# Layer norm statistics finished on GpSimd, and normalized tiles transposed by DMA, in a one-core transformer block

## The chip, the cores and the metric

The kernel runs on one core of a Trainium2 chip. The time is device microseconds (us) of that core for one execution. TensorE is called PE, VectorE DVE, ScalarE ACT, GpSimd POOL and SyncE SP, as in the profile.

## What is computed

One block of an adaptive layer norm transformer over 2048 tokens of width 512, in bf16. Six vectors come from a conditioning vector; the first half is a sliding-window attention of 32 heads of width 16 with a window of 256 tokens, the second half an MLP that mixes over tokens.

```python
mod = (silu(c) @ w_mod).reshape(1, 6, 1, -1)            # sa, ca, ga, sb, cb, gb
h = layernorm(x) * (1 + ca) + sa                        # eps 1e-5 under the root
q, k, v = split_heads(h @ wqkv)                         # 32 heads of 16
p = softmax(where(0 <= i - j < 256, q @ k.T * 16**-0.5, -1e9))
x = x + ga * ((p @ v) @ wo)
h = layernorm(x) * (1 + cb) + sb
h = layernorm(h)
u = gelu(einsum('bsd,sf->bdf', h, w1) + b1)             # f = 1792, sums over tokens
x = x + gb * (einsum('bdf,fs->bds', u, w2) + b2).T
```

## The kernel before, in words

The 2048 tokens lie in 16 tiles of 128 tokens by 512 features (`xres`, tile x in the profile). They form four groups G of four tiles. For each group the kernel does three things.

**Projection** (`proj0` for group 0, `proj(G)` from line 875 for groups 1 to 3). `norm_ops` (line 621) takes the statistics of the four tiles: for each tile a BATCH_NORM_STATS2 and a BATCH_NORM_AGGREGATE on DVE, which leave mean and variance in mv; then, for the batch of four, two ACT instructions that make rs = exp(-0.5 ln(var + eps)); then, where `shifted` is set, one DVE instruction for nm = -mean * rs. `normalize` (line 653) makes xn = x * rs + nm on POOL. Then `e_tr` (line 909) transposes xn on PE, 16 blocks of 128x128 for a group, into two PSUM tiles pt, and `e_h` (line 919) evicts them with scale and shift of the modulation into h1T, four instructions of 128x512, on ACT or DVE. There is one h1T, so a group's transposes stand behind the last projection matmul of the group before (`before`). Projection matmuls give pq, pk, pv; DVE or ACT evicts these to QT, kb and vb, and POOL spreads kb and vb into KT and VT with masks.

**Attention** (`attention`, line 1166). 75 chunks of scores. A chunk is 512 columns for each of four heads: scores on PE into pss (three heads, 1536 columns) and psb (the fourth), two exponentials on ACT into et (128x1536 and 128x512), a mask product on DVE, and products with VT and with ones on PE into po. ACT makes the reciprocal of the sums (two instructions on lz), and DVE the product OT. Seven et tiles form a ring.

**Post** (`post`, line 1058). The output projection pa, the sum with x, and the two layer norms of the second half (tags l2 and l3) with the modulation between them, down to hb, the input of the MLP. Groups 0 to 2 take batches of four tiles and normalize on POOL; group 3 takes two batches of two tiles on DVE.

The MLP's first matmul sums over tokens. For the first eight tiles it is done during attention (`partials`, line 1128: 14 sums of eight matmuls, kept in part), for the other eight in `tail` (line 1332); the second matmul py follows (line 1398). The first halves of w1 (seven transfers of 512 KB, tiles w1p) are loaded together once the modulation's tiles are released; the second half of a pair is loaded into the same tile when the first is used up. w2 (14 transfers of 512 KB, w2r) goes into the room that attention leaves. All these transfers are issued in order by SP.

**What sets the order.** Each step is an `Op` with engines, a cost and a place `pos`. `run_schedule` (line 157) is a list scheduler that runs when the program is built: it picks, step by step, what can start first by the costs written in the code, and emits it; each engine then runs its instructions strictly in that order. The table `MOVED` shifts the place of each step, `CHOSEN` pins some steps to an engine, and a few constants set tolerances. Three PSUM banks (od0 to od2) are shared by all matmul results except the scores. Nearly every instruction is recorded with one source line, L321, that of the helper `wrapped`, so the profile is read by tile names.

Of the kernel before, what the change touches and what calls it, by code (L numbers as in the profile page):

```python
# [9 lines left out]
ACT = mybir.ActivationFunctionType  # L10
# [49 lines left out]
    70, 4467, 3352, 236, -2676, 456, 1177, 4380, -3616, 1904, 51, -1450, 1581, 958, 823, -389, -5421, -5059, 1961,  # L60
    2253, 438, -1893, -2821, 945, -1140, -4188, -353, -2060, -2167, -978, 2785, -3149, 1766, 1833, 1121, 397, -1610,
    2266, -135, 1589, -377, 7177, -547, -1613, 2278, 49, -3915, -2041, 1444, 697, 2329, 335, 842, -1466, -1538,
    1377, -5151, -700, -1478, -1297, -2245, -1441, -577, -782, -322, 1149, 2468, -1282, -23, -9, -2034, -1112,
    -2090, -625, 418, 4015, -42, 441, -1267, 2114, -2423, -17, -1812, 180, 3007, -20, -127, 802, 3660, -1718, -5323,
    3891, -7996, 648, -157, -307, -3897, 3154, -248, -205, -746, -758, -341, -1065, -1027, -4094, -1115, -563, 774,
    -567, 919, -3068, -612, 3429, -533, -2943, -2732, -468, 0, 0, 0, -2833, 0, 0, 0, 4012, 0, 0, 0, 2087, 0, 0, 0,
    -2967, 0, 0, 0, 1896, -3625, -4555, -4396, -1330, -4146, -5997, 945, -4357, -2281, -2265, -4078, -3736, -2234,
    -2238, -2088, -5933, -6820, -1831, -3919, -86, 0, 0, 0, 2917, 0, 0, 0, -3397, 0, 0, 0, -3869, -126, -4012,
    -3163, -3098, -2291, -4626, 0, 0, 0, -3744, 0, 0, 0, -1255, -4473, -1567, -5495, -1964, -1985, 265, 0, 0, 0,
    918, 0, 0, 0, -4777, 0, 0, 0, 1884, -2580, -2329, -6050, -3851, -5651, 256, 0, 0, 0, -5949, 0, 0, 0, -4823,  # L70
    -7822, -188, -4690, -2183, -263, 1168, -1223, 183, -640, -1307, -1147, -1714, -1455, -1506, -2586, 369, 1115,
    1706, -2188, -2861, 3663, 4317, -1900, -3694, -32, 3684, -759, -1106, 3652, 3201, 467, 894, -202, 3287, -1972,
    1847, -2954, -7238, 4109, 577, -2623, 1009, 1661, 161, -2100, 101, -2459, -3002, 5002, -912, -1539, -2952, -188,
    -1212, -4900, -1081, -1401, -1012, -4700, -847, -478, -927, -4723, 4, -2646, -2959, 1376, -2654, 2541, -1668,
    1670, -4531, 263, 242, -1454, -761, 5658, 701, -1595, -1229, 6812, 142, 3436, -1137, -1827, 1368, -8297, -973,
    4089, 270, -301, 1175, 1887, 356, -1883, 3294, 2057, -2871, -6721, 1015, -3531, 3626, -577, 0, 0, 0, 2127, 0, 0,
    0, -2754, 0, 0, 0, -4673, 943, -6490, -2346, -6169, 6023, -570, 0, 0, 0, -2772, 0, 0, 0, -4887, -5214, -7251,
    -5132, -1166, -2049, -1760, 0, 0, 0, -1967, 0, 0, 0, -5431, 0, 0, 0, -3239, -3416, -1061, -5548, -213, 83,
    -2126, 0, 0, 0, 3863, 0, 0, 0, -4984, -5944, -9389, -5675, -2048, -16, -1222, 0, 0, 0, -5372, 0, 0, 0, 2682, 0,
    0, 0, -617, -2090, -6144, -7478, -6129, -2188, -1303, 0, 0, 0, 696, 0, 0, 0, -1038, -2636, -6267, -1648, -1777,  # L80
    2198, 1755, 0, 0, 0, 492, 0, 0, 0, -1432, 0, 0, 0, -1277, -2134, -6449, -2845, -3570, -2232, -1708, 0, 0, 0,
    -6073, 0, 0, 0, 1239, -2264, -6809, -228, -8212, -689, -989, -6426, -3078, 2186, 337, -1300, 1261, -2087, -2761,
    893, 177, -1261, 2307, 1095, -2051, 2155, 1484, -718, -1829, -3249, 2311, -1384, 4273, -2313, 3194, -1649, 1588,
    1454, 5130, -530, -710, -982, 2509, -101, -180, 1765, 2456, 1338, 1123, -3497, 463, 3176, 4783, -112, -2629,
    -3687, -4796, -2110, 1941, 3875, -3895, -2150, -1119, 511, 1867, 2651, -2030, 286, -1797, 2014, -2735, -3109,
    -6218, 5379, -1878, -1972, 2969, 669, -1488, -1885, 5494, 5382, 2803, 1178, 419, 210, 665, -1845, -2987, -1371,
    -2546, -79, 502, 2421, -3740, -3509, -4120, 3194, 1449, 2377, 7205, 1978, -4180, 1689, 328, 595, 861, -1145, 0,
    0, 0, -1748, 0, 0, 0, -3812, 0, 0, 0, -852, -2397, -8784, -7079, -5062, -2663, -5549, 0, 0, 0, -1775, 0, 0, 0,
    -2167, -4070, 1863, -11014, 1648, -2508, -3414, 0, 0, 0, -9171, 0, 0, 0, 1351, 0, 0, 0, -3992, -8907, -294,
    -2896, -1484, -1986, -3310, 0, 0, 0, -1995, 0, 0, 0, -8063, -3126, 497, -7719, -3726, -818, -3217, 0, 0, 0,  # L90
    -2662, 0, 0, 0, -2304, 0, 0, 0, -2693, -3688, -2743, -9195, -2877, -2467, -3147, 0, 0, 0, 596, 0, 0, 0, -1887,
    -9586, -8234, -8156, -458, -1239, -6090, 0, 0, 0, -1663, 0, 0, 0, 529, 0, 0, 0, -935, -8603, 1013, -8474, -4906,
    5740, -3352, 0, 0, 0, -1917, 0, 0, 0, -180, -5566, -5089, -12042, -481, 6294, -3974, -1183, -3266, -178, -1697,
    -6917, -619, -5490, -2874, 2307, -5558, -1283, -4286, 97, 688, 6764, -1, -1859, -415, 3548, 1772, -4681, 1128,
    -2098, -2960, 1273, -1577, -163, 2239, 2964, 5783, 4456, -4137, -1579, 46, 0, -1588, 934, -546, -666, -3967,
    922, 13, 3137, 4633, 2039, 3624, 1927, -1697, 1288, 2451, 2284, 960, -220, 1747, -1705, 1834, -14, -324, -1715,
    930, 5465, 2964, 3593, 1371, 13, -2362, 3398, 338, -227, -500, 2508, 2181, -2169, 2677, -444, 743, 735, 1245,
    255, -2098, 430, 1563, -3647, 2858, 1753, 2806, 527, -3215, 2354, 512, 815, -1559, -5022, 401, -899, 2225, -711,
    0, 0, 0, -3379, 0, 0, 0, -8261, 0, 0, 0, -3454, -2109, -10884, -12007, -4125, -741, -1625, 0, 0, 0, -8786, 0, 0,
    0, -2529, -1969, 877, 2220, -3540, -689, -4323, 0, 0, 0, -2887, 0, 0, 0, 3442, 0, 0, 0, 1147, -506, -4707, 243,  # L100
    -4008, 4990, 538, 0, 0, 0, -1551, 0, 0, 0, 801, 2579, -669, -851, 595, -1406, -3620, 0, 0, 0, 1957, 0, 0, 0,
    4432, 0, 0, 0, -592, -548, -329, -509, -4812, 2495, -5021, 0, 0, 0, -6650, 0, 0, 0, -1072, 1375, -5880, -5071,
    -2736, 3118, 1549, 0, 0, 0, 2386, 0, 0, 0, -3661, 0, 0, 0, 477, 1221, -1627, -2365, -361, 5951, 594, 0, 0, 0,
    2506, 0, 0, 0, 3581, -1001, 1296, 176, 420, 397, 324, -4889, -2563, -1105, -2612, -2591, -604, -599, -862, 1146,
    -1278, 2218, -1316, 2057, 3521, 4902, -1209, -814, 1554, -2807, -2931, -1068, 3534, -141, -4935, -918, 93,
    -4825, 5353, 376, 1479, 227, -286, 525, -4654, 286, -1945, -1026, -5792, 2309, -1932, 2357, -6381, -4690, -6370,
    2678, 1440, -1714, -5050, 2763, 2858, -5925, -3043, 29, 2732, 665, -5900, 1821, 446, 1510, -2919, -7548, -1921,
    1301, 2643, 494, -5402, -1795, 1683, 1622, 2097, -6974, -1007, 1550, 1919, 2660, 71, -1309, 1458, 2205, -6599,
    826, -804, 1417, 1615, -4471, 2083, -3678, 1073, 3010, 1306, 433, -3422, 1315, 1609, -1032, -411, 78, 1524,
    1477, -6392, -434, 3787, 1105, 5774, -5290, 1101, -1493, -4202, 968, 1042, -54, -172, -4572, -3764, 2523, -765,  # L110
    2726, 2606, 5637, -466, 2597, 3103, 823, 5349, 4113, -246, 101, 1017, -4325, -5010, 4065, 5501, -473, 1661,
    -3058, 2980, -6736, 4775, -848, 3670, 2893, 1742, 2902, -1577, 4555, 2286, 3783, 2751, 1785, 1240, -4116, 3712,
    -1835, 5125, 2811, 1922, -734, -3129, 2641, -2571, 5041, -405, -1849, 1660, -1257, 3386, -2559, 1378, -2067,
    182, -112, -909, 3526, -424, 1530, 2954, -307, 2441, -3570, 3799, 3287, -2833, 2974, -2740, 1418, -1497, 4010,
    -5506, 2265, -2370, -187, 4427, -970, 2987, 4216, 210, -2930, 1810, 1023, 5420, 3094, 6105, 3490, 2010, -2298,
    -2949, -4217,
]
CHOSEN = {
    "ACT": [
        80, 91, 111, 116,  # L120
    ],
    "DVE": [
        65, 73, 75, 78, 83, 87, 100, 106, 109, 114, 276, 280, 287, 295, 299, 310, 313, 317, 498, 501, 516, 520, 528,
        542, 723, 726, 737, 748, 752, 767, 938, 943, 953, 958, 968, 973, 978, 998,
    ],
}
S_TOL = 0.154
E_TOL = 0.474
LATE = 2.695
BATCH = True  # L130
HORIZON = 202.566
STICK = 5.96
AV_POS = 0.2
LZ_POS = 0.0
M_POS = -0.5
OT_POS = -1.0
FINE = 0.0


# [140 lines left out]
def kernel(  # L280
# [340 lines left out]
    def norm_ops(tag, tiles, deps, poss, key, shifted):  # L621
# [27 lines left out]
        if shifted:  # L649
            o = op(f"{tag}nm", "DVE", 0.12, e_nm, deps=[o], pos=poss[-1])  # L650
# [793 lines left out]
```

## Time and profile before

| | |
|---|---|
| time, median of 3 runs (lowest to highest) | 264.41 us (264.3 to 265.02) |
| time of the profiled execution | 264.88 us |
| its span, first to last instruction | 263.1 us |
| first exponential starts, last one ends | 12.9 us, 181.8 us |
| first matmul of py starts | 211.1 us |

The profile lists, for each engine, busy time, groups of like instructions (count, busy us, mean ns), what ended an engine's idle time, and a chain of waits that leads back from the last instruction. Instructions of one engine overlap a little at their ends, so the sum of means is somewhat above the busy time, and the distance from one start to the next is what an instruction really takes from its engine. Three stretches are told apart below: up to 13 us (loads, modulation, first projection), 13 to about 180 us (attention with all else beside it), and the rest (the MLP).

### The profile page before, as it was taken

Reading aid. Unit: us, or ns where it says so; the run is one execution under the profiler, and the core shown is the slowest. Engines: PE = TensorE matmul, PEld = TensorE weight load, DVE = VectorE, ACT = ScalarE, POOL = GpSimd, SP = SyncE. Lnnn points to the kernel's source line nnn. Section 1 sums busy time; section 2 is a strip of 40 time slices with the busy share of each in tenths; the row PEclk is TensorE's granted clock in tenths of the full one; section 3 lists DMA queues with packets and bytes.
Section 4 is the critical chain, followed back from the end, with each engine's and each line's share of the span. In section 5 each row is a group of like instructions: output and inputs, shape, how many; then the busy total and the mean of one; then the engine's idle time right before and its main releaser. Section 6 shows DMA issues by size and latency. Waiting matters only on the chain.

```text
span 263.1 us, 8290 instructions
## 1 busy us (share of the span) xinstructions
PE 238.3 (91%) x3568; PEld 130.6 (50%) x3605; DVE 209.9 (80%) x438; ACT 183.5 (70%) x273; POOL 91.3 (35%) x129
## 2 busy tenths in 40 slices
PE   8889879899986898878899999999999999999994
PEld 2666556554654444444644444446444444444441
DVE  3799999998999989999856979789778864444443
ACT  3499999999998998998999999997226620000000
POOL 5069903970796692387840051050000000000000
PEclk9999999999999999999999999999999999999999
DMA  7999100099000000000002022222699501111111
GB/s 220 319 350 235 4 4 2 3 278 264 23 4 2 2 2 2 2 2 1 5 2 82 1 82 82 85 80 82 229 383 386 201 23 40 41 40 55 47 40 40
DMA packets 33261, 24.66 MB, mean 94 GB/s; under 512 B 5064, under 2 KB 29640, under 8 KB 33224
## 3 DMA queue, kind: packets, MB, share of 16 engines
q1 hardware_dynamic: 32800, 23.74, 29.9%
q8 instruction: 28, 0.46, 0.7%
q10 hardware_dynamic: 424, 0.39, 0.4%
q14 instruction: 9, 0.07, 0.1%
HBM read 22.03 MB, written 2.10 MB: 92 GB/s over the span
## 4 chain that ended last, share of the span: by engine, by line
DVE 39%; PE 33%; ACT 16%; issue 7%; DMA 3%; SPq 0%; DVEq 0%
PE py L321 18%; ACT et L321 13%; PE pu L321 10%; DVE et L321 10%; DVE st L321 7%; DVE h L321 4%; DVE vb L321 3%; DVE kb L321 3%; ACT lz L321 2%; DVE OT L321 2%; DVE QT L321 2%; DVE x L321 2%; DVE h1T L321 2%; DMA x<-in_A_x_dram 2%; PE po L321 2%
## 5 line engine op out<-in xcount | busy, mean ns | idle before, releaser
L321 ACT ACTIVATE et<-pss 128x1536 bf16<-128x1536 f32 x75 | 109.4, 1458 | 3.6 <-PE psb L321 2.7
L321 DVE TENSOR_TENSOR et<-et,maskt 128x1024 bf16<-128x1024 bf16 (+1 forms) x79 | 49.6, 635 | 6.9 <-ACT et L321 6.5
L321 PE MATMUL pu<-hb,w1p 128*128 128x512 bf16 x212 | 50.2, 380 | 1.0 <-issue 0.8
L321 PE MATMUL py<-guT,w2r 128*128 128x512 bf16 x220 | 48.3, 379 | 0.2
L321 ACT ACTIVATE et<-psb 128x512 bf16<-128x512 f32 x75 | 45.5, 607 | 0.0
L321 POOL TENSOR_SCALAR KT<-kb,mask_par 128x512 bf16<-128x512 bf16 (+1 forms) x38 | 27.5, 736 | 37.0 <-DVE kb L321 36.9
L321 PE MATMUL pss<-QT,KT 32*128 32x64 bf16 (+3 forms) x720 | 29.9, 230 | 7.6 <-ACT et L321 4.7
L321 PEld LDWEIGHTS <-w2r 128*128 128x128 bf16 x224 | 21.9, 98 | 26.4
L321 PE MATMUL po<-et,VT 128*32 128x64 bf16 (+3 forms) x960 | 32.0, 234 | 3.0 <-DVE kb L321 2.1
L321 POOL TENSOR_SCALAR xn<-x,rs,nm 128x512 bf16<-128x512 bf16 x24 | 24.0, 1006 | 28.5 <-DVE nm L321 26.1
L321 PEld LDWEIGHTS <-w1p 128*128 128x128 bf16 x224 | 20.2, 98 | 24.9 <-issue 2.4
L321 PE MATMUL po<-et,ones_bd 128*32 128x256 bf16 (+3 forms) x624 | 31.4, 268 | 0.0
L321 DVE TENSOR_TENSOR otile<-py,xr 128x512 bf16<-128x512 f32 x16 | 11.1, 692 | 25.5 <-PE py L321 25.5
L321 PEld LDWEIGHTS <-KT 32*128 32x128 bf16 x960 | 16.6, 92 | 28.5 <-issue 25.5
L321 PE MATMUL psb<-QT,KT 32*128 32x64 bf16 (+3 forms) x240 | 29.3, 231 | 0.0
L321 POOL TENSOR_SCALAR VT<-vb,mask_half 128x512 bf16<-128x512 bf16 x32 | 25.9, 823 | 5.9 <-DVE vb L321 5.4
L321 PEld LDWEIGHTS <-VT 128*32 128x32 bf16 x960 | 20.3, 96 | 10.6 <-issue 7.8
L321 DVE BATCH_NORM_STATS2 st<-x 128x6 f32<-128x512 bf16 x32 | 22.0, 686 | 3.1 <-DMA x<-in_A_x_dram 2.8
L321 PEld LDWEIGHTS <-wqkv 128*128 128x128 bf16 x164 | 14.1, 97 | 16.7 <-issue 8.2
L321 PE MATMUL pk<-h1T,wqkv 128*128 128x256 bf16 (+1 forms) x98 | 19.7, 319 | 2.2 <-DVE QT L321 1.7
L321 PE MATMUL pv<-wqkv,h1T 128*64 128x256 bf16 x256 | 17.2, 275 | 1.1 <-DVE h1T L321 0.5
L321 PE MATMUL pa<-wod,OT 128*128 128x512 bf16 x57 | 15.9, 381 | 0.7 <-DVE wod L321 0.2
(83 smaller groups left out, 288.5 us busy)
## 6 DMA issues: line engine op xcount, KB each, us to landing
w1p<-in_B_w_dram SPq DMA_DIRECT2D x14, 512.0 KB, 5.7
w2r<-in_B_w_dram SPq DMA_DIRECT2D x14, 512.0 KB, 10.8
wmod<-in_w_mod_dram SPq DMA_DIRECT2D x4, 512.0 KB, 8.3
out_dram<-otile SPq DMA_DIRECT2D x16, 128.0 KB, 1.7
x<-in_A_x_dram SPq DMA_DIRECT2D x15, 128.0 KB, 5.2
wqkv<-in_A_wqkv_dram SPq DMA_DIRECT2D x4, 256.0 KB, 5.4
wmod<-in_w_mod_dram SPq DMA_DIRECT2D x3, 256.0 KB, 4.5
wqkv<-in_A_wqkv_dram SPq DMA_DIRECT2D x1, 512.0 KB, 5.8
```

The costliest lines, as they stand in the source:

```text
L321: ins = call(*args, **kwargs)
```

## The change

Five things change together.

1. In batches of four tiles (`quiet`: tag l1 of groups 1 to 3, tags l2 and l3 of groups 0 to 2, nine batches) DVE does only BATCH_NORM_STATS2. The aggregate, the two ACT instructions and nm are gone; seven small POOL instructions on 128x4 or 128x8 make mean and 1/sqrt(var + eps) out of the raw statistics, the last by a power of -1/2. `normalize` then does (x - mean) * rs, still one POOL instruction.
2. In groups 1 to 3 the transposes on PE and the evictions are gone. Four DMA transposes of 128x512, issued by SP, write h1T, and `e_h` applies scale and shift in place in SBUF, on DVE or POOL. There are two h1T tiles, used by turns, so a group waits for the projection two groups before.
3. The loads of w1's first halves are seven steps of their own, each placed by the scheduler, and so are the loads of the second halves.
4. `warm` moves to another pool, three small memsets are added on POOL, some buffer counts change.
5. The tables `MOVED` and `CHOSEN` and the scheduler's constants are replaced, so the order of the instructions on all engines is a new one.

```diff
-    def norm_ops(tag, tiles, deps, poss, key, shifted):
+    def norm_ops(tag, tiles, deps, poss, key, quiet):
...
-            st = small.tile([P, nc.vector.BN_STATS_DIM], F32, name="st", tag=tag + "st")
-            ve.bn_stats(out=st[:], in_=tiles(i)[:])
-            ve.bn_aggr(out=box[key][0][:, i, :], in_=st[:])
+                box[key] = new("st", 6), new("mv", 2), new("rs")
+            st, mv = box[key][0][:, i, :], box[key][1][:, i, :]
+            ve.bn_stats(out=st, in_=tiles(i)[:])
+            if not quiet:
+                ve.bn_aggr(out=mv, in_=st)
+
+        def e_ag(e):
+            st, mv, rs = box[key]
+            sq = small.tile([P, n], F32, name="sq", tag=f"sq{n}", bufs=2)
+            po.tensor_tensor(out=mv[:], in0=st[:, :, 1:3], in1=st[:, :, 4:6], op=ALU.add)
+            po.tensor_tensor(out=mv[:], in0=mv[:], in1=halves[:, 0:n, :], op=ALU.mult)
+            po.tensor_tensor(out=sq[:], in0=st[:, :, 1], in1=st[:, :, 4], op=ALU.subtract)
+            po.tensor_tensor(out=sq[:], in0=sq[:], in1=sq[:], op=ALU.mult)
+            po.tensor_scalar(out=sq[:], in0=sq[:], scalar1=0.25, scalar2=EPS, op0=ALU.mult, op1=ALU.add)
+            po.tensor_tensor(out=sq[:], in0=sq[:], in1=mv[:, :, 1], op=ALU.add)
+            po.tensor_tensor(out=rs[:], in0=sq[:], in1=power[:, 0:n], op=ALU.pow)
...
-        def e_nm(e):
-            mv, rs, nm = box[key]
-            ve.scalar_tensor_tensor(out=nm[:], in0=mv[:, :, 0], scalar=-1.0, in1=rs[:], op0=ALU.mult, op1=ALU.mult)
...
-        o = op(f"{tag}rs", "ACT", 0.45, e_rs, deps=st_ops, pos=poss[-1])
-        if shifted:
-            o = op(f"{tag}nm", "DVE", 0.12, e_nm, deps=[o], pos=poss[-1])
-        return o
+        if quiet:
+            return op(f"{tag}ag", "POOL", 2.0, e_ag, deps=st_ops, pos=poss[-1])
+        return op(f"{tag}rs", "ACT", 0.45, e_rs, deps=st_ops, pos=poss[-1])
...
-            a = op("tr", "PE", 0.27, lambda e, f=e_tr: f(0), deps=xn_ops[0:2], pos=p_tr, cls="D", alloc="od", behind=before)
-            z = op("tr", "PE", 0.27, lambda e, f=e_tr: f(1), deps=xn_ops[2:4] + [a], pos=p_tr, cls="D")
-                h = op("h1T", {"ACT": 1.0, "DVE": 0.9}, 0.9, e_h, deps=[z, o_fm] + before, pos=p_tr)
+        h1T = h1Ts[r2]
+        before = [proj_last[G - 2]] if G >= 2 else []
...
+        def e_xt(e, i):
+            dma.dma_start(out=h1T[:, :, i * P : (i + 1) * P], in_=xn[i][:], transpose=True)
...
+            xt_ops.append(op("xt", "SP", 1.25, lambda e, i=i: e_xt(e, i), deps=xn_ops[-1:] + before, pos=p_ln + 2.5, extra=XT_AFTER))
...
+                for dc in (2 * dp, 2 * dp + 1):
+                    ENGINE[e].tensor_scalar(
+                        out=h1T[:, dc, :], in0=h1T[:, dc, :], scalar1=scale, scalar2=shift, op0=ALU.mult, op1=ALU.add,
+                    )
+            h_ops.append(op("h1T", {"POOL": 1.85, "DVE": 0.66}, 0.9, e_h, deps=xt_ops + [o_fm], pos=p_tr))
...
-        for pair in range(NF // 2):
-            load_w1(pair, 0)
...
+            loaded.append(op("w1l", "SP", 1.35, lambda e, n=n: load_w1(n, 0), deps=loaded[-1:] or [opened],
+                             pos=start_of(1) + 3.0 + 2.0 * n, extra=W1_AFTER))
...
-                if fc % 2 == 1:
-                    load_w1(fc // 2, 1)
...
+            if fc % 2 == 1:
+                second[fc // 2] = op("w1h", "SP", 1.35, lambda e, fc=fc: load_w1(fc // 2, 1), deps=[g], pos=pos + 0.5, extra=W1_AFTER)
```

## The prediction

> **What bounds the kernel now.** First the busy time by stretches: start and end, length, then busy us of PE, PE's weight loads, DVE, ACT and POOL.
>
> ```profile
> 13.00:140.00 127.00, 110.56 (x2319) 68.37 (x2338) 118.66 (x246) 121.84 (x176) 79.76 (x98) 1.00 0.24 62
> 140.00:180.00 40.00, 38.19 (x700) 19.71 (x710) 34.34 (x74) 39.70 (x58) 7.93 (x8) 1.00 0.26 74
> 180.00:211.00 31.00, 30.61 (x258) 14.92 (x251) 26.21 (x59) 15.53 (x29) 0.00 (x0) 1.00 0.74 265
> 211.00:263.00 52.00, 48.44 (x222) 21.83 (x224) 23.13 (x36) 1.27 (x2) 0.00 (x0) 0.99 0.12 41
> ```
>
> From 13 to 180 us ACT is busy for 161.5 of 167 us: this stretch is as long as ACT's work plus 5.5 us. DVE comes second (118.7 of 127 up to 140). After 180 PE works without a gap, and its clock row reads full. So the time is a start of 13 us, ACT's work, and a run of PE at the end. What ended ACT's idle time inside the stretch (us, times, longest):
>
> ```profile
> ACT et L321 <- PE psb L321: 2.7, 6, 0.8
> ACT rs L321 <- DVE mv L321: 0.7, 2, 0.5
> ACT lz L321 <- PE po L321: 0.6, 2, 0.4
> ```
>
> Little of it is anyone's fault; the work itself has to go. The groups by shape (count, busy us, mean ns, idle before):
>
> ```profile
> L321 ACT ACTIVATE rs<-mv,eps_t 128x4 f32<-128x4 f32 x9 | 2.9, 317 | 0.7 <-DVE mv L321 0.7
> L321 ACT ACTIVATE rs<-rs 128x4 f32<-128x4 f32 x9 | 1.9, 206 | 0.3
> L321 DVE BATCH_NORM_AGGREGATE mv<-st 128x2 f32<-128x6 f32 x48 | 8.7, 182 | 1.7
> L321 DVE TENSOR_SCALAR h1T<-pt,modFM 128x512 bf16<-128x512 bf16 x12 | 5.9, 534 | 0.0
> L321 DVE SCALAR_TENSOR_TENSOR nm<-mv,rs 128x4 f32<-128x4 f32 x9 | 1.9, 213 | 1.1 <-ACT rs L321 1.1
> L321 POOL COPY maskt<-tmpm 64x64 bf16<-64x64 bf16 x6 | 1.3, 250 | 0.0
> ```
>
> The first two rows are the change's target on ACT: 18 instructions of four columns each, 4.8 us. What they take from ACT is read from starts in the timeline:
>
> ```profile
> 172.52 0.35 ACT L321 ACTIVATE rs<-mv,eps_t 128x4 f32<-128x4 f32 x1
> 172.90 0.21 ACT L321 ACTIVATE rs<-rs 128x4 f32<-128x4 f32 x1
> 173.01 1.43 ACT L321 ACTIVATE et<-pss 128x1536 bf16<-128x1536 f32 x1
> ```
>
> The pair begins at 172.52 and the next exponential at 173.01: 0.49 us.
>
> **The change, part by part.**
>
> *ACT.* Nine pairs go: 9 x 0.49 = 4.4 us. In the changed order three evictions QT of 128x256 (386 ns by their row) stand on DVE and not on ACT; instructions of this size start 0.27 us apart (lz at 161.43, the next at 161.70), so 0.8 us more. ACT's work falls by **5.2 us**, nearly all of it ahead of the 54th exponential (136.5 us). The order of scores and exponentials is otherwise the same, and the count of partial sums ahead of the last scores too (102 matmuls before, 98 after).
>
> *DVE.* 36 of the 48 aggregates go (36 x 0.182 = 6.6), nine nm (1.9) and the twelve evictions of pt (12 x 0.534 = 6.4). Added are three QT of 128x256 (1.2 us at 0.40) and eight in-place products on h1T, the other four being on POOL. That shape and pair of operations stands in the row xn of group 0 at 428 ns; 406 is its value without POOL beside it, and 918 the slowest DVE instruction on 128x512 in SBUF (one wod). I take 428: 3.4 us, within 3.2 to 7.3. Sum: -6.6 - 1.9 - 6.4 + 1.2 + 3.4 = **-10.3 us**, or -6.4 at the worst. DVE falls well behind ACT, so none of this counts by itself; it hides the added work and may take some of ACT's 5.5 us of idle time.
>
> *PE.* 48 transposes go: by the row of pt (56 in 4.8 us) 4.1 us. PE is 87% busy up to 140, so this too is relief, not gain.
>
> *POOL.* 9 x 7 small instructions. Nothing in the trace has this size on POOL but memsets of 128x2 (102 ns) and the copy of 64x64 (250 ns), and no power at all; ends are 63 x 0.10 = 6 us and, at the 554 ns of KT on 128x256, 35 us. I take 250, the nearest with an input: 15.8 us, 1.75 us a batch. With four h1T at 841 ns (KT of 128x512) POOL gains 19 us, 15.7 of them up to 140: 95 of 122 us busy. POOL has the room. Behind each batch stand the spreads KT and VT, which PE waits for; but the path from the last statistics to xn gets no longer, since it loses the wait in ACT's queue (24.49 rs, 25.13 nm).
>
> *DMA transposes.* No row shows one. Each moves 128 KB. The nearest: stores of 128 KB land after 1.7 us, loads of x of 128 KB after 5.2 beside other traffic, and SP needs 0.37 us to issue one. In the stretch where group 1 needs them the DMA row of the page reads 1, then 0, so I stay near the stores: 2.5 us each, overlapping; ends are 1.7 us for all and 4 x 5.2 in a row. Before, xn of group 1 runs on POOL from 29.59 to 33.04 and h1T from 35.43 to 37.6; with 2.5 us the last tile lands at about 36, so nothing changes. Groups 2 and 3 have more air: h1T in two copies lets their transposes run a group earlier. On SP they stand behind b2b (issued by 26.1) and ahead of the first loads of w1 (51.5), which partial sums need only after 120 us.
>
> The Trainium skill's page DMA: Bandwidth & Descriptors (Latency and other measured facts; Anatomy of one DMA) gives 261 GB/s for transposes and about 2 us fixed; by these an estimate is 0.5 + 2.0 = 2.5 us, and no run here shows it yet. The sum stays as it is.
>
> *The start.* Three memsets (0.1 us each) precede the identity on POOL; DVE waits 2.8 us for x there, which hides them. *The end.* In the changed order the second half of the last w1 pair is issued behind all 14 loads of w2, where before it was third. Before, the first w2r goes out at 184.94, when the last po is done, and fifteen transfers of 0.52 MB at the page's 383 GB/s take 20.5 us. PE has 106 matmuls, 0.219 us each (49 in 10.74), between the last po and the first that reads this tile: 23.2 us. It just fits, so 0 us.
>
> **Sum.** The profiled execution took 264.9 us (its span 263.1 and 1.8 around it). Less 5.2 of ACT's work and 0.3 of its 0.7 us of waits for mv: 259.4. The median lies 0.5 below the profiled execution, so **259.0 us**. Kept idle time on ACT is my choice: it could fall by up to 5 us, with DVE relieved, or rise.
>
> **Rivals.**
>
> *More than the work.* With 10 us less on DVE and 4 on PE the waits for psb, pss and po (3.8 us) go too: 255.5. Against it: PE is the one waited for there, and its order with the new transposes is no simpler.
>
> *GpSimd slows DVE.* The products with bc_sb on tile h, all of one shape:
>
> ```profile
> L321 DVE TENSOR_TENSOR h<-h,bc_sb x13: 424/714/880, 73.2 to 179.7; 128x512 bf16<-128x512 bf16 x13
> ```
>
> They take 424 ns at least and 880 at most, and the long ones (0.80 at 73.17, 0.88 at 75.50) lie while POOL runs xn and VT; POOL's KT in turn needs 690 to 1197 ns. POOL's share up to 140 rises from 63% to 78%: some 80 products in SBUF on DVE, 0.15 more of them covered, 0.37 us each: 4.4 us, of DVE's 10.3. DVE keeps 6 us of relief, so ACT should stay the limit; but DVE ran at 98% up to 56 us, and there stalls may eat half the gain: 261.7. The Trainium skill speaks against this change here: GPSIMD Engine Reference (Performance versus the Vector engine; Key points) holds elementwise work on GpSimd to be about twice as slow and in contention with VectorE; the trace agrees on the contention.
>
> *The last tile of w1 is late.* If w2 lands at 300 GB/s, or its issue is held by the queue, PE waits at the end: fifteen transfers take 26 us, 3 more than PE has: 262.
>
> *Slower: group 1 stalls.* In the changed order the four in-place products of group 1 stand together in DVE's queue, waiting for all four transposes; masks, OT and evictions to free the three PSUM banks queue behind them. If transposes run one after another at 5.2 us, the last lands at 30.4 + 21 = 51 and not 37, and DVE stands for 13 us in a stretch where it has no slack. The same holds if the batch of seven takes many us on POOL. Group 1's first scores come at 48, its keys are ready at 41.9, so up to 5 us are absorbed; the rest, 8 us or more, is lost: 267. It decides from about 3.3 us a transpose in a row. For it: nothing here shows a transposing transfer; against it: no traffic beside them, and stores of the same size land in 1.7 us.
>
> **How the numbers follow.** Forecast (257 to 261) 0.60; more than the work 0.07; GpSimd slows DVE 0.12; late w1 tile 0.07; group 1 stalls 0.14. The likeliest gives 259.0. From 256.0 to 263.7 lie all but the last and some of the second: 0.82. A measurement of this kernel tells 0.3%, 0.8 us, from no change. Faster is the first four, less 0.05 that ends within 0.8 us of 264.4: 0.80; with 0.01 of the last, same is 0.06; slower 0.14.
>
> **What would show it.** Right: ACT has no rs of 128x4, its busy time falls by 6 and the last exponential ends near 176.5; DVE falls by about 10; POOL rises by 15 to 25. Transposes: landing under 3 us, no wait of DVE's h1T for DMA over 1 us. The end: no wait of PE's pu for w1p. Wrong: idle ACT over 7 us up to the last exponential, DVE's masks and h much longer than now, or h1T waiting.

## The result, and the profile after

The changed kernel takes **293.3 us** (median of 4 runs, 293.14 to 294.45) where the kernel before takes 264.36 beside it: a ratio of 1.110, interval 1.107 to 1.113. Forecast were 259.0 us, with a range up to 263.7; the forecast has the wrong sign and misses by 34 us. Where a kernel has executions over 1.5% above its fastest one, a median below is over all its executions and a ratio over the others. The profiled execution took 293.41 us, its span 291.7, and the mean clock of TensorE is 0.952 where it was 0.999.

The same stretches as before, columns as there (PE, PEld, DVE, ACT, POOL, then clock, DMA share, GB/s):

```profile
13.00:140.00 127.00, 102.52 (x2028) 60.02 (x2044) 106.72 (x199) 105.99 (x141) 120.82 (x141) 0.95 0.31 74
140.00:180.00 40.00, 34.25 (x636) 17.17 (x637) 22.70 (x42) 33.29 (x46) 21.17 (x21) 0.91 0.15 42
```

POOL, busy 79.8 us of the first 127 before, is now busy for 120.8, while ACT stands at 106 where it was at 121.8. POOL is now the busiest engine up to 140 us. The chain of waits, by engine, says the same; before it held no POOL at all (DVE 39%, PE 33%, ACT 16%):

```profile
POOL 39%; PE 31%; DVE 14%; DMA 7%; issue 4%; ACT 3%; POOLq 1%; SPq 0%
```

What ended ACT's idle time (us, times, longest); the three rows answer to those for psb, po and pss before, which had 0.8 us at the longest:

```profile
ACT et L322 <- PE psb L322: 19.1, 10, 6.1
ACT lz L322 <- PE po L322: 11.8, 6, 7.3
ACT et L322 <- PE pss L322: 5.9, 1, 5.9
```

These are 37 us in 17 waits. Sixteen of them, 29.5 us, lie ahead of the last exponential, which ends at 202.6 us, 20.8 later than before. The longest, 7.3 us, lies behind it: POOL makes four hb from 198.1 to 206.8, a matmul pu waits 3.8 us for them, and the last products po are queued behind pu. The first matmul of py starts at 239.8, 28.7 later.

What POOL does with its time, by shape (count, busy us, mean ns, idle before), first the kernel before, then the changed one:

```profile
L321 POOL TENSOR_SCALAR xn<-x,rs,nm 128x512 bf16<-128x512 bf16 x24 | 24.0, 1006 | 28.5 <-DVE nm L321 26.1 <-DVE h L321 2.5
L321 POOL TENSOR_SCALAR hb<-h,rs,nm 128x512 bf16<-128x512 bf16 x12 | 10.8, 909 | 13.9 <-DVE nm L321 13.9
```

```profile
L322 POOL TENSOR_SCALAR xn<-x,mv,rs 128x512 bf16<-128x512 bf16 x24 | 53.4, 2230 | 0.2
L322 POOL TENSOR_SCALAR hb<-h,mv,rs 128x512 bf16<-128x512 bf16 x12 | 25.4, 2127 | 0.2
L322 POOL TENSOR_TENSOR rs<-sq,power 128x4 f32<-128x4 f32 x9 | 10.0, 1111 | 0.7
```

The rows xn and hb matter most: the 36 normalizations of the same tiles go from means of 1006 and 909 ns to 2230 and 2127. They have the same shape, the same engine and the same operation name; POOL spends 44 us more on them. The rows of the small instructions add up to 23.6 us, the power being the largest.

The clock falls where PE stands still. A gap in PE's work and the stretches behind it, columns as above:

```profile
124.00:126.00 2.00, 0.00 (x0) 0.00 (x0) 0.70 (x1) 1.22 (x2) 2.00 (x3) 1.00 0.00 0
126.00:128.00 2.00, 0.00 (x0) 0.00 (x0) 1.97 (x5) 0.00 (x0) 2.00 (x2) 0.82 0.00 0
130.00:132.00 2.00, 2.00 (x50) 1.27 (x52) 2.00 (x4) 0.93 (x1) 2.00 (x2) 0.50 0.00 0
```

How POOL's lateness gets to PE is seen in the timeline, DVE first:

```profile
125.30 0.91 DVE L322 TENSOR_TENSOR h<-xn,bc_cb 128x512 bf16<-128x512 bf16 x1 [4.33 <-POOL xn L322]
127.90 0.67 DVE L322 CAST QT<-pq 128x512 bf16<-128x512 f32 x1
```

```profile
128.62 1.01 PE L322 MATMUL pk<-h1T,wqkv 128*128 128x512 bf16 x2 [4.84 <-DVE QT L322]
```

DVE stands 4.3 us ahead of a product on xn that POOL is still making; the eviction QT, whose matmul was long done, is queued behind it, and PE's next matmuls wait for QT. Then PE works for some 5.5 us at half of the clock. So a long wait such as this one is paid a second time.

### The profile page after: what moved, and what is told of

The parts are those of the page before. It is cut to its first block, busy times and chain, and to the rows that moved or that the text cites. A ratio compares the mean times of both kernels' runs of the same rounds, so it can differ in the third digit from the quotient of the medians.

```text
span 291.7 us, 8238 instructions
## 1 busy us (share of the span) xinstructions
PE 245.9 (84%) x3518; PEld 129.0 (44%) x3557; DVE 205.2 (70%) x392; ACT 179.1 (61%) x252; POOL 161.4 (55%) x199
## 4 chain that ended last, share of the span: by engine, by line
POOL 39%; PE 31%; DVE 14%; DMA 7%; issue 4%; ACT 3%; POOLq 1%; SPq 0%
PE py L322 17%; POOL xn L322 12%; PE pu L322 9%; POOL hb L322 8%; POOL VT L322 5%; POOL KT L322 5%; DMA w1p<-in_B_w_dram 4%; DVE st L322 3%; POOL rs L322 3%; DVE et L322 3%; POOL sq L322 3%; DVE h L322 3%; PE po L322 3%; ACT et L322 2%; DMA x<-in_A_x_dram 2%
## 5 line engine op out<-in xcount | busy, mean ns | idle before, releaser
L322 PE MATMUL pu<-hb,w1p 128*128 128x512 bf16 x213 | 55.1, 401 | 10.4 <-POOL hb L322 7.9
L322 POOL TENSOR_SCALAR xn<-x,mv,rs 128x512 bf16<-128x512 bf16 x24 | 53.4, 2230 | 0.2
L322 PE MATMUL pss<-QT,KT 32*128 32x64 bf16 (+3 forms) x720 | 31.2, 236 | 11.1 <-POOL KT L322 4.7
L322 PE MATMUL po<-et,VT 128*32 128x64 bf16 (+3 forms) x960 | 34.1, 243 | 6.9 <-DVE part L322 2.2
L322 PEld LDWEIGHTS <-w1p 128*128 128x128 bf16 x224 | 20.9, 101 | 37.9 <-issue 15.5
L322 PE MATMUL po<-et,ones_bd 128*32 128x256 bf16 (+3 forms) x624 | 32.8, 280 | 0.0
L322 POOL TENSOR_SCALAR KT<-kb,mask_par 128x512 bf16<-128x512 bf16 (+1 forms) x38 | 26.8, 718 | 9.0 <-DVE kb L322 8.5
L322 PE MATMUL psb<-QT,KT 32*128 32x64 bf16 (+3 forms) x240 | 30.7, 237 | 0.0
L322 PEld LDWEIGHTS <-VT 128*32 128x32 bf16 x960 | 20.4, 100 | 17.2 <-issue 12.9
L322 PE MATMUL pk<-h1T,wqkv 128*128 128x256 bf16 (+1 forms) x98 | 21.3, 340 | 5.2 <-DVE QT L322 4.8
L322 POOL TENSOR_SCALAR hb<-h,mv,rs 128x512 bf16<-128x512 bf16 x12 | 25.4, 2127 | 0.2
```

Source lines behind the costliest of these rows:

```text
L322: ins = call(*args, **kwargs)
```

## The experiments

**Theory:** the two operations of the normalization are what costs. Before, POOL computes x * rs + nm (multiply, add); now (x - mean) * rs (subtract, multiply), and POOL is slow at that. **Rivals:** the batch of seven on POOL, the DMA transposes, or the new order.

### 1. The old form of the normalization, in the changed kernel

```diff
-    nc.gpsimd.memset(halves[:, :, 0], 0.5)
+    nc.gpsimd.memset(halves[:, :, 0], -0.5)
...
+            po.tensor_tensor(out=nm[:], in0=mv[:, :, 0], in1=rs[:], op=ALU.mult)
...
+                out=dst, in0=src, scalar1=rs[:, i : i + 1], scalar2=nm[:, i : i + 1], op0=ALU.mult, op1=ALU.add,
```

> The changed kernel, with POOL's normalization written as x * rs + nm again: the mean is kept negated, and an eighth small POOL instruction makes nm = -mean * rs. All else, order included, stays. Theory F (the form: subtract-then-multiply takes 2.06 us on POOL where multiply-then-add took 0.76, and a full POOL delays everything): POOL busy falls from 161 to about 118 us, the time to 257 to 262 us. Rival O (the new order, and seven small POOL instructions of 2.8 us a batch ahead of KT and VT, are what makes POOL late): still 280 us or more. Rival T (the wait for transposes on DVE, 3.5 us, and what queues behind it): 275 us or more.

Measured: 264.58 us, ratio to the kernel before 0.995 (0.992 to 0.999). POOL's busy time falls from 161.4 to 121.7 us, and xn and hb are back at 954 and 875 ns. All of the loss was the form: 28.7 us by these medians, so rivals O and T are out. What was not as expected is the other end: 257 to 262 us were expected, and no gain of 5 us is left.

### 2. The new form, in the kernel before

```diff
-                out=dst, in0=src, scalar1=rs[:, i : i + 1], scalar2=nm[:, i : i + 1],
-                op0=ALU.mult, op1=ALU.add,
+                out=dst, in0=src, scalar1=mv[:, i, 0:1], scalar2=rs[:, i : i + 1],
+                op0=ALU.subtract, op1=ALU.mult,
```

> The kernel before, its order and its instructions kept, but the 36 normalizations on POOL written as (x - mean) * rs; nm is still made and not read. Theory F: each takes about 2.06 us, 36 x 1.2 = 43 us more on POOL, which was idle for 47 of 127 us up to 140; what it hides is little, as the normalizations come in fours: 275 to 292 us. Rivals O and T: the form costs little by itself, 264 to 268 us.

Measured: 278.39 us, ratio 1.050 (1.046 to 1.054). The form alone costs 13.6 us in the old order, and it does so with the old statistics, transposes and queues; xn and hb have means of 2159 and 2130 ns. Up to 140 us POOL is busy for only 99.6 of 127 us, and yet ACT's waits for psb and pss grow from 3.2 to 13.8 us: the long instructions cost where they are waited for, though POOL is not full. In the changed kernel, where POOL carries the statistics too, the form costs twice as much; that the statistics are the reason was not tested.

### 3. Same count of instructions, add in place of subtract

The mean is stored with its sign turned (the first line of experiment 1), and the normalization becomes (x + (-mean)) * rs. Against the changed kernel nothing else differs, not even the number of instructions.

```diff
-            out=dst, in0=src, scalar1=mv[:, i, 0:1], scalar2=rs[:, i : i + 1], op0=ALU.subtract, op1=ALU.mult,
+            out=dst, in0=src, scalar1=mv[:, i, 0:1], scalar2=rs[:, i : i + 1], op0=first, op1=ALU.mult,
```

(`first` is `ALU.add` on POOL.)

> The changed kernel with the mean kept negated and POOL's normalization written as (x + nmean) * rs: as many instructions as in the change, add in place of subtract. If subtraction is the slow part: as the kernel with multiply-then-add, 257 to 262 us. If any pair but multiply-then-add is slow: 290 to 296 us, as the change. Rival O: 290 us or more whatever the form.

Measured: 263.81 us, ratio 0.995 (0.992 to 0.998). The groups by shape of this kernel:

```profile
L322 POOL TENSOR_SCALAR xn<-x,mv,rs 128x512 bf16<-128x512 bf16 x24 | 23.2, 974 | 2.5 <-DVE h L322 2.3
L322 POOL TENSOR_SCALAR hb<-h,mv,rs 128x512 bf16<-128x512 bf16 x12 | 10.5, 889 | 0.2
```

One word, subtract for add, is 45 us of these two rows (41 of POOL's whole busy time, as other rows got longer) and 29.5 us of the kernel. The order of operations is not what costs. The time lies above the 257 to 262 us that were expected, as in experiment 1.

### 4. The forms by themselves

A kernel that leaves the whole block out and runs only pairs of operations on tiles of 128x512 in bf16, on POOL and on DVE, alone and beside each other (`a`, `b` are scalars in SBUF).

```python
forms = [("mulAdd", ALU.mult, ALU.add, a, b), ("subMul", ALU.subtract, ALU.mult, a, b),
         ("addMul", ALU.add, ALU.mult, a, b), ("mulSub", ALU.mult, ALU.subtract, a, b), ...]
```

> Not the block: it leaves the whole computation out and copies x to the output, but for one tile. POOL alone runs eight pairs of operations on 128x512 in bf16, three times each, then a product and powers of -1/2 on 128x4 in f32; then DVE products run beside POOL in each of the two forms. Theory F: multiply-then-add 0.76 us, subtract-then-multiply about 2.06 us with nothing beside it. Rival (contention): both take about 0.77 us alone, and subtract-then-multiply is long only beside DVE. For power: 1.0 to 1.1 us, 0.8 more than a product.

Measured, one row each (count, busy us, mean ns):

```profile
L50 POOL TENSOR_SCALAR mulAddb<-x,sc 128x512 bf16<-128x512 bf16 x1 | 0.8, 792 | 0.0
L50 POOL TENSOR_SCALAR addMulb<-x,sc 128x512 bf16<-128x512 bf16 x1 | 0.8, 762 | 0.0
L50 POOL TENSOR_SCALAR subMulb<-x,sc 128x512 bf16<-128x512 bf16 x1 | 2.1, 2067 | 0.0
L50 POOL TENSOR_SCALAR mulSubb<-x,sc 128x512 bf16<-128x512 bf16 x1 | 2.1, 2066 | 0.0
```

A subtract in either place makes the instruction 2.7 times as long (the first row ran beside DVE; multiply-add with DVE idle took 762 to 768 ns). It is neither the order of the two operations nor the operands: add and multiply in the same order, with the same scalars, take 762 ns, and with constants the pair with subtract still takes 1.92 us. DVE makes no such difference: its fastest are 401 ns with the subtract and 411 without, its others 704 to 858 in both forms, all of them beside POOL's work. The power of -1/2 on 128x4 takes 1.00 us, a product of this size 0.19.

### 5. The last tile of w1 ahead of w2

What was left open: with the fast form the forecast's 5 us should have come, and 1.0 came (263.81 us against 264.81 of the kernel before beside it). In experiment 3 the last exponential ends at 178.7 us, 3.1 earlier than before, but the first matmul of py starts at 211.6, 0.5 later. So the gain was given back behind attention. SP's queue in experiment 3 (start, us, issue):

```profile
181.38 11.99 SPq L1311 DMA_DIRECT2D w2r<-in_B_w_dram  x14
194.40 0.73 SPq L1101 DMA_DIRECT2D w1p<-in_B_w_dram  x1
```

And its windows there:

```profile
200.00:204.00 4.00, 3.95 (x19) 1.76 (x18) 2.89 (x8) 2.16 (x4) 0.00 (x0) 1.00 1.07 363
204.00:206.00 2.00, 0.27 (x2) 0.00 (x0) 2.00 (x6) 1.57 (x3) 0.00 (x0) 1.00 0.40 97
208.00:210.00 2.00, 2.00 (x6) 0.73 (x5) 0.06 (x1) 0.00 (x0) 0.00 (x0) 0.51 0.00 0
```

PE has nothing from 204.3 to 206.4, until the tile is there, and then runs six matmuls in two us where it ran ten: the clock reads 0.51. The experiment issues this one load when the first of w2 goes out:

```diff
     def e_w2(e):
+        load_w1(NPART // 2 - 1, 1)
         att.close()
```

> The changed kernel with normalization as (x + (-mean)) * rs (263.81 us), and one transfer moved on SP: the second half of the last w1 pair is issued ahead of the 14 loads of w2 and not behind them. In the profile of the version without this move PE waits 2.1 us for this tile at 204 us, and then runs from 206 to 209.9 us at half of the clock, which costs 1.9 us more. Theory (the relief of ACT is real and is given back at this wait): the wait and the slow clock both go, py starts near 207.7 us, and the time falls by 4.0 to 259.8 us. Rival 1 (only the wait itself goes, the clock falls for another reason): 261.7 us. Rival 2 (the end is bound by the transfers of w2 in any case): 263.8 us.

Measured: **260.87 us**, ratio 0.987 (0.984 to 0.990), faster than both kernels. SP's queue (behind one load of w2, at 180.75 us) and the same stretches now:

```profile
181.66 0.37 SPq L1101 DMA_DIRECT2D w1p<-in_B_w_dram  x1
182.09 13.54 SPq L1312 DMA_DIRECT2D w2r<-in_B_w_dram  x13
```

```profile
204.00:206.00 2.00, 2.00 (x11) 0.88 (x10) 2.00 (x6) 1.47 (x3) 0.00 (x0) 1.00 0.07 28
208.00:210.00 2.00, 2.00 (x11) 0.93 (x10) 1.58 (x4) 0.64 (x1) 0.00 (x0) 1.00 0.02 4
```

No gap, full clock, py from 206.9: 4.2 us earlier than in the kernel before, 4.7 earlier than in experiment 3 (0.6 of this is an earlier start of attention). That the end is bound by w2 is out. The time alone lies between theory (259.8) and rival 1 (261.7); it is the profile that shows both the wait and the slow clock gone. Against experiment 3 the median falls by 2.9 us and not by 4.0. This fits the clocks: most executions of experiment 3 had kept theirs, those with a mean clock of 1.00 with spans of 261.1 to 262.2, those at 0.994 (the profiled one too) 263.5 and 263.6. In experiment 1 the profile puts a wait of 2.2 us at the same place down to the tile a on DVE, though the load stood at the end of the queue there too: a name in the list of waits is a hint, and moving the load is the test.

### 6 to 8. Each part alone, in the order of the kernel before

Part 1 alone: the batch of seven stands on POOL where ACT's pair stood, and the order of all other instructions is that of before. The line that places it (the batch itself is that of the change, with the mean negated):

```diff
-        o = op(f"{tag}rs", "ACT", 0.45, e_rs, deps=st_ops, pos=poss[-1])
+        o = op(f"{tag}rs", "ACT", 0.45, e_ag if shifted else e_rs, deps=st_ops, pos=poss[-1])
```

> The kernel before, its order kept on every engine, with part 1 of the change alone: in the nine batches the aggregates, the two ACT instructions and nm go, and the batch of seven runs on POOL at the place where ACT's pair stood; normalization is (x + (-mean)) * rs, the fast form. Theory (the stretch up to 180 us is as long as ACT's work): ACT loses 9 x 0.49 = 4.4 us, the last w1 tile is third in SP's queue as before, so nothing is given back: 260.0 us. Rival (the batch takes 3.0 us on POOL and not 1.2 on ACT and DVE, and what stands behind it on POOL comes late): part of the 4.4 us turns into waits of ACT for PE, 262 to 265 us.

Measured: 267.8 us, ratio 1.011 (1.009 to 1.014): slower, and beyond what either expectation allowed. ACT's pairs are gone, but its waits in attention grow (2.7 and 0.6 before), and a wait of 2.4 us on lz, put down to b2FM on DVE, is new:

```profile
ACT et L321 <- PE psb L321: 4.1, 7, 1.2
ACT lz L321 <- PE po L321: 2.7, 3, 1.2
```

Up to the last exponential (185.3 us, 3.5 later) ACT is idle for some 12 us in place of 5.5. The list of waits points at POOL's VT and KT behind the batch: DVE waits 2.8 us for VT where it evicts into vb, PE 1.8 us for KT, and neither wait is there before. PE gaps of 2 us are followed by a stretch at 0.63 of the clock (86 to 90 us). What each of these costs was not separated.

Part 2 alone: each xn is transposed by a DMA issued right behind it, and the evictions become products in place. Two h1T and four xn tiles (five before) are taken over from the changed kernel.

```diff
             normalize(e, xn[i][:], xres[4 * G + i][:], ("l1", G, i0), i - i0)
+            dma.dma_start(out=h1T[:, :, i * P : (i + 1) * P], in_=xn[i][:], transpose=True)
```

> The kernel before, its order kept, with part 2 of the change alone: the 48 transposes on PE go, each xn of groups 1 to 3 is transposed by a DMA that is issued right behind it, and the twelve evictions become twelve in-place products on DVE. Statistics and normalization as before. Theory (ACT's work sets the length, and ACT loses nothing here): 264.8 us, within 0.8. Rival 1 (4 us less on PE and 1 to 2 on DVE shorten ACT's waits): 261.5 to 263.5 us. Rival 2 (2.4 us of landing stands in the path from xn to the first projection, where PE's transposes took 1): 266 us or more.

Measured: 269.39 us, ratio 1.017 (1.015 to 1.019); the time is that of the rival with the landing in the path, but what the trace shows is a queue. In the order of before group 2's transposes stand on SP behind seven loads of w1 (52.0 to 62.5 us). The row of SP, then DVE's first product of that group with the wait ahead of it, then PE's windows:

```profile
62.56 11.30 SPq L898 DMA_TRANSPOSE h1T<-xn  x5
```

```profile
72.65 1.52 DVE L321 TENSOR_SCALAR h1T<-h1T,modFM 128x512 bf16<-128x512 bf16 x3 [2.97 <-DMA h1T<-xn]
```

```profile
70.00:72.00 2.00, 0.21 (x8) 0.00 (x0) 0.00 (x0) 2.00 (x4) 2.00 (x4) 1.00 0.66 27
74.00:76.00 2.00, 1.77 (x16) 1.20 (x16) 1.43 (x4) 0.00 (x0) 0.00 (x0) 0.50 0.27 54
```

The four xn of this group are ready at 58.1 us, 4.5 ahead of the first issue; transposes land up to 5.9 us after theirs; PE stands for 4 us and then has half of the clock. The run with these loads out of the way was not made.

Both parts, in the order of before:

> Both parts together in the order of the kernel before (fast form of normalization; the w1 loads as before). If the parts add up, the time is that of the run with part 1 alone plus the difference that part 2 alone makes, 259 to 261 us by the theory that ACT's work sets the length. If the new order is what earns the gain, this is slower than the changed order with the early w1 tile by 1 us or more; if the old order is as good, the two are within 0.8 us.

Measured: 275.29 us, ratio 1.041 (1.039 to 1.044): 10.7 us slower, where the two parts alone add up to 8.1. By the theory of ACT's work it should have been 259 to 261; it fails here. The same two parts in the changed order, with the fast form and the early tile, take 260.87. So the parts earn nothing in the order of before, and the gain needs the changed order (with its loads of w1 placed one by one); whether that order would gain without the parts was not run.

## Why the prediction was wrong, point by point

- **POOL** is the step that failed: "95 of 122 us busy. POOL has the room." This sum counts the small instructions and four h1T. For the 36 normalizations it keeps the old duration ("still one POOL instruction", as the change's description has it) and so puts the new pair of operations at nothing, without a reason, though the diff shows it. Measured: 36 instructions of 2.2 us for 0.97, 44 us more; POOL is busy for 120.8 of 127 us up to 140, and 28.7 to 29.5 us of the kernel's time hang on this term (experiments 1 and 3). Nor does a share of busy time give the price, as experiment 2 shows.
- *The small instructions.* Forecast 15.8 us at 250 ns, 1.75 a batch; measured 23.6, and 3.0 from the first start to the end (25.71 to 28.73) in the first batch. Six of seven lie at 221 to 347 ns, so 250 was near; the power at 1.11 us was not. Once the form was fast, POOL was busy for 102.9 of 127 us up to 140 (experiment 5), near what was forecast, and the loss was gone.
- *ACT.* Forecast -5.2. In experiment 5, where nothing hides it, ACT's busy time between the first exponential's start and the last one's end falls from 163.4 to 159.4, so -4.1: the pairs went as counted (one of 128x2 is left there) and QT too, but three more instructions on lz stand ahead of the last exponential, and the exponentials' means are 8 ns longer, 150 times. Idle time stayed (5.5, now 5.8), as chosen. The last exponential ends at 178.1, 3.7 us earlier, where 5.3 was forecast.
- *DVE and PE.* Forecast -10.3 and -4.1. Measured in experiment 5: -7.4 and -3.5. Neither shortened ACT's waits.
- *DMA transposes.* Forecast 2.5 us; measured a median of 2.4 and 3.8 at most in the changed kernel, where DVE waited for them once, 3.5 us (0.5 in experiment 5). The Trainium skill's page DMA: Bandwidth & Descriptors (Latency and other measured facts; Anatomy of one DMA), from which an estimate of 2.5 us stood beside it, agrees with the trace. What the term lacked is their place: 1.2 us each of SP's time, and behind other loads up to 5.9 us to land (experiment 7).
- *The start.* As forecast: first exponential at 12.9 us in experiment 5, 13.1 in the changed kernel.
- *The end.* "It just fits, so 0 us" was wrong. PE's 23.2 us were right (23.0 in experiment 3, from the last po to the gap), but the fifteen transfers took 25.0 and not 20.5 us (181.4 to 206.4): the core's traffic was 115 GB/s from 180 to 184 us and 270 from 184 to 188, and 363 to 401 only after that. The rival "late w1 tile", at 26 us, had the size. It left out that PE's clock halves behind the gap. The changed kernel has the wait too, 1.5 us.
- *Rival "GpSimd slows DVE".* Small. The sixteen products with bc_sb have a mean of 578 ns before, 629 in the changed kernel and 578 in experiment 5; the medians (426, 754, 427) jump because about half of the products are long in each. This is 0.9 us of DVE's work in all.
- *Rival "group 1 stalls".* Right in sign, wrong in mechanism and size, and in part in place. Group 1's four xn, with two VT between them, take POOL from 29.65 to 40.2 us, where they took 3.5 us before; the transposes add at most that wait of 3.5 us. But of ACT's 29.5 us of waits ahead of the last exponential 8.5 lie up to 60 us and 15 behind 120.
- *More than the work.* Did not occur: idle time on ACT did not fall.
- *Two slips of reading.* POOL's KT on 128x512 ran 685 to 1367 ns, not 690 to 1197; and the first four chances less 0.05 give 0.81 for faster, which leaves 0.13 for slower. Neither bears on the forecast.

With the fast form and without the late tile, the kernel takes 260.87 us, inside the forecast's 257 to 261. That does not prove the sum. Experiment 6 takes the same pairs off ACT in the old order: ACT's work up to the last exponential falls by 2.8 us (163.4 to 160.7), and its idle time grows by 6.3. Keeping the idle time was, as the prediction says, a choice; it held in the changed order and failed in the old one, and why is not shown. Of the 1.9 us between 259.0 and 260.87, 1.2 lie in the span, which fell by 4.3 and not by 5.5 (1.1 of ACT's work and 0.6 of its idle time, less some gain behind attention); the rest is that this median lies 0.3 above its profiled execution, where the forecast put it 0.5 below.

What is open: whether a faster batch of statistics (the power alone is 1.1 us of it) would gain more, and what the changed order would be worth without part 1 or part 2. Neither was tried. Why POOL takes so much longer with a subtract is open too; the runs show that it does.

## What to carry to other kernels

Compare the operations inside an instruction, not its name and shape: where a diff alters the pair of operations on GpSimd, no row of the profile before prices it, and the range has to say so. Here storing the negated mean and adding it costs no instruction. A moved load is priced against what lies ahead of it in its queue from that queue's own start. A gap on TensorE can cost more than its length, as it did here.

## What the runs showed of the hardware

GpSimd's TENSOR_SCALAR on 128x512 bf16, with scalars in SBUF, takes 0.76 us with add and multiply, 0.79 to 0.93 beside VectorE's work; with a subtract in it 2.07 us, and up to 2.30 beside VectorE's (experiment 4). The Trainium skill's page GPSIMD Engine Reference (Performance versus the Vector engine; Key points) holds elementwise work there to be about twice as slow as on VectorE; the runs agree for add and multiply (0.76 us to 0.41 at the fastest on VectorE), but with a subtract it is five times (2.07 to 0.40).

The slow form contends less with VectorE: beside a stream of multiply-add on POOL a DVE product takes 764 ns on average, beside subtract-multiply 550 (experiment 4).

TensorE's clock fell to 0.50 after a gap of only 2.1 us (204.26 to 206.40 in experiment 3) and stayed there for 3.4 us (206.5 to 209.9). After 4.8 us without a matmul in the changed kernel it was at 0.50 for 6.8 us (127.3 to 134.1), after 4 us in experiment 7 for 6.8 as well (73.7 to 80.5). Six of the ten executions of experiment 3 had a mean clock of 1.00; whether they had the gap, no trace shows. The Trainium skill's page TensorE: Matmul & The Clock Gate (Part 1: The HAM clock gate) gives the half rate after an idle window of about 3.4 us that runs free, and the full rate after a busy window as long; the 0.50 and the stretches of 3.4 us and twice that agree with these traces, the length of the gap that suffices does not.
